# Pooling the opening's chunks in another way: strided reductions, split loads and a new order

## The chip, the cores and the metric

The kernel runs on one core of one Trainium2 chip. The metric is the device time of one execution in microseconds; several executions are timed and their median is given. A separate profile of one execution supplies the trace that the text reads: what each engine did, when, and what it waited for. The engines are TensorE (PE, with its weight loads as PEld), VectorE (DVE), ScalarE (ACT), GpSimd (POOL) and SyncE (SP), which here only issues transfers.

## The reference

An attention with spatially reduced keys is followed by a gated feed-forward layer:

```python
# q (4, 12288, 128), kv (4, 384, 32, 128), w_sr (128, 128)
kv_pool = kv.reshape(B, H // 4, 4, W // 4, 4, C).mean(axis=(2, 4))
k = v = kv_pool.reshape(B, -1, C) @ w_sr            # 768 keys for each image
s = (q @ k.transpose(0, 2, 1)) / np.sqrt(C)
a = softmax(s)                                       # over the 768 keys
x = (a @ v).reshape(B * N, 128)                      # 49152 tokens
out = (np.maximum(x @ w_gate, 0) * (x @ w_val)) @ w_out   # d_ff = 1536
```

Everything is float32 at the boundary; the kernel works in fp16 behind the loads and accumulates in fp32.

## The kernel before

The 49152 tokens are cut into 96 tiles of 512. The keys of an image are pooled in six chunks of 128 keys each; two chunks make a pair, and a pair is loaded as four lines (line dh holds the rows with that offset in the 4x4 pooling window; each partition gets 2 chunks x 4 pixels x 128 channels). One key of a chunk is thus the sum of 16 pieces: 4 lines x 4 pixels.

A tile goes through scores (TensorE), exponentials (ScalarE), values times weights (TensorE), 12 value projections `v`, 12 gate projections `g`, their copies `y` (value out of PSUM, ScalarE) and `h` (ReLU gate times value, VectorE), and 12 output matmuls `o`. From tile 4 on, a loop runs over the tiles as a pipeline; in each round a list of words (FIRST, then STEADY, at the end DRAIN and LAST) gives the order of the steps. The schedule is manual: each engine executes its instructions in the order in which the words issue them, and semaphores hold an engine until its operands are there.

The first four tiles (0 to 3, `LEAD`) and the keys of image 0 are made in the opening, the list OPENING, one call of `open_step` for each word. A dot separates two numbers. The words that matter here:

- `aJ`, `bJ`, `cJ`: sum two lines of chunk J, then add a third, then a fourth (512 elements a partition, `sum_lines`). `pJ`: sum pixels 0 and 1 with 2 and 3 (`sum_pixels`).
- `TJ.n`: TensorE turns the four pixels of line n of chunk J and adds them into one PSUM bank (`turn_add`; a matmul against the identity, so turning and adding is one step, 4 instructions); `TJ.p` does so with the two pieces left by `pJ`.
- `kvTJ`: the turned chunk is copied to SBUF; `pjJ`: projection by w_sr; `keyJ`: the keys scaled to fp16; `vtJ`, `valJ`: the same turned back as values.
- `castI`, `qtI`, `qTI`: a q tile cast to fp16, turned on TensorE, copied from PSUM; for tiles 4 and 5 the turn is a transposing transfer on SP's queue.
- `Sk.J`: scores of tile k against chunk J (one 512-wide matmul) and their exponential on ScalarE. `Vk.J`: the values of chunk J times these weights, added into tile k's bank. `xTk`: that bank copied out as fp16.
- `U0`, `U1`: matmuls with ones give the row sums of the four tiles, 24 matmuls of 32 columns each in all; `R`: VectorE transposes these sums and inverts them, and GpSimd copies the squares into `lead_scale`, 16 copies. `lead_scale` is needed when the output of tile 0 is scaled, near the end of the first round of the loop.
- `v0.n`, `g0.n` (tile 0): value projection with its copy, gate projection with its gate.
- `gateN`, `W0`, `W1`, `wo`: GpSimd waits for line N mod 4 of chunk N / 4, then issues the loads of the feed-forward weights.

ENGINES names the engine of a step (a ScalarE, v VectorE, p GpSimd; VectorE where nothing is named). PSUM has eight banks, taken from a list and given back in the order of the words (`bank`, `freed`, line 107); an instruction that writes a bank waits for the last reader of its former contents. The last words of OPENING may take only six banks, since the other two become the wide score bank of the loop. Before the opening, `fill(5)` runs five fp32 matmuls on the identity while the first lines are under way (L615).

Loads are issued in this order on SP's queue (lines 1 and 3 of pair 0 on ScalarE's): the lines of pair 0, w_sr, q tiles 0 and 1, line 0 of pair 1, q tiles 2 and 3, lines 1 to 3 of pair 1, the four lines of pair 2, q tiles 5 and 4. An issue waits for the landing of the transfer eight before it. After OPENING, GpSimd reads the last gated block of tile 0 into `gate` (L699) and issues the q loads of group 2 (L144).

Of the kernel before, what the change touches and what calls it, by code (L numbers as in the profile page):

```python
# [9 lines left out]
FP32 = mybir.dt.float32  # L10
FP16 = mybir.dt.float16
AF = mybir.ActivationFunctionType
ALU = mybir.AluOpType
# [3 lines left out]
def kernel(  # L17
# [48 lines left out]
    ENGINES = dict(word.split(":") for word in """  # L66
        key0:a val0:a a1:p kvT1:a key1:a val1:a key2:a val2:a a3:p b3:p p3:p kvT3:a val3:a
        cast0:a cast1:a qT1:a cast3:a cast4:p cast5:p xT1:a xT3:a
    """.split())
    OPENING = """  # L70
        T0.1 T1.3 cast1 T0.3 cast0 T1.2 T0.2 a1 p1 T1.p T0.0 kvT1 kvT0 pj1 qt1 pj0 T2.0 qT1 a3
        key1 cast3 qt0 cast2 vt1 qT0 key0 S1.1 qt2 qt3 qT2 val1 qT3 S1.0 S0.1 T2.1 S0.0 vt0 val0
        V1.1 S2.0 b3 c3 S2.1 S3.0 S3.1 T2.2 V0.1 T2.3 V1.0 kvT2 V2.1 V0.0 p3 gate22 W0 W1 cast4
        qT4 wo cast5 qT5 pj2 V2.0 T3.p T5.0 key2 vt2 kvT3 val2 pj3 key3 S0.2 T5.1 vt3 val3 S2.3
        a4 S0.3 S1.2 S2.2 T5.2 V0.2 S3.2 b4 V2.3 T5.3 V0.3 c4 S1.3 kvT5 S3.3 pj5 p4 T4.p V1.2
        key5 kvT4 V1.3 S0.5 pj4 key4 S2.5 vt5 val5 V2.2 S0.4 vt4 val4 S2.4 V0.5 V3.0 S1.4 V0.4
        S3.4 xT0 S1.5 V2.5 V2.4 S3.5 xT2 v0.5 g0.5 U0 v0.2 U1 v0.0 R g0.2 v0.3 V1.4 V3.1 g0.0
# [19 lines left out]
    """.split()  # L97
    SUMS = [{}, {"a": [0, 1]}, {}, {"a": [0, 1], "b": ["s", 2], "c": ["s", 3]}, {"a": [0, 1], "b": ["s", 2], "c": ["s", 3]}, {}]

# [16 lines left out]
    def freed(ps):  # L116
        free_banks.append(bank_numbers.pop(id(ps))[0])
        return ps
# [90 lines left out]

    def kv_load(b, pair, lines=range(r), queues=(nc.sync,)):  # L210
# [12 lines left out]
        rows = kv[b, pair * 2 * HC : (pair + 1) * 2 * HC].rearrange(  # L223
            "(hp dh) (wp h dw) c -> dh hp wp (h dw c)", dh=r, h=2, dw=r
        )
        for dh in lines:
            queues[dh % len(queues)].dma_start(
                parts[dh].rearrange("p h dw c -> p (h dw c)"), rows[dh]
            )

# [16 lines left out]
    def line(chunk, dh):  # L247
        return kv_in[0, chunk // 2][dh][:, chunk % 2]
# [3 lines left out]
    def add(name, to, x, y):  # L252
        engine_of(name).tensor_tensor(to, x, y, op=ALU.add)
# [6 lines left out]
    def sum_pixels(name, chunk):  # L260
        s1 = sums.pop(chunk)
        pixels[chunk] = work.tile([128, 2, C], FP32, tag="kv_c2", bufs=2, name="kv_c2")
        add(name, pixels[chunk], s1[:, 0:2], s1[:, 2:4])

    def turn_add(chunk, lines):
# [72 lines left out]
    hTs, o_banks, o_sbs, vals = {}, {}, {}, {}  # L338

    def scores(k, jc):  # L340
        if k not in aTs:
            aTs[k] = work.tile([128, NJC, T], FP16, tag="aT", bufs=AT_BUFS, name="aT")
        s_ps = bank([128, T])
        nc.tensor.matmul(s_ps, kv16[:, k // NST, jc, 0:C], qT_of(k), start=True, stop=True)  # L344
        nc.scalar.activation(aTs[k][:, jc, :], freed(s_ps), AF.Exp, scale=qk_scale)

# [79 lines left out]

    def lead_sums(chunks):
        if "sums" not in x_banks:
            x_banks["sums"] = bank([128, T])
        for jc in chunks:  # L430
            for k in range(LEAD):
                nc.tensor.matmul(  # L432
                    x_banks["sums"][32 * k : 32 * (k + 1), :], ones, aTs[k][:, jc, :],
                    start=jc == 0, stop=jc == NJC - 1, skip_group_check=True,
                    tile_position=(0, 32 * k),
                )

    def lead_scales():
# [21 lines left out]
    def keep_value(k, fb):  # L460
        vals[k, fb] = work.tile([128, T], FP16, tag="val", bufs=6, name="val")
        (nc.vector.tensor_copy if k < LEAD - 1 and fb == 5 else nc.scalar.copy)(  # L462
            vals[k, fb], freed(proj_banks.pop(("v", k, fb)))
        )
# [125 lines left out]

    w_sr_f32 = const.tile([128, C], FP32)
    kv_load(0, 0, range(r), (nc.sync, nc.scalar))
    nc.sync.dma_start(w_sr_f32, w_sr)
    q_load_pair(0)
    kv_load(0, 1, range(1))
    q_load_pair(2)
    kv_load(0, 1, range(1, 4))
    kv_load(0, 2)
    q_load_tile(5)
    q_load_tile(4)  # L600

# [16 lines left out]

    fill(5)
    freed(idle)  # L620

    gate = const.tile([128, 1], FP32)
    done = set()

    def open_step(word):
        head = "T" if word[0] == "T" else word.rstrip("0123456789.")
        at = [int(x) for x in word[len(head):].split(".") if x] if head != "T" else []
        if head in ("a", "b", "c"):
# [5 lines left out]
        elif head == "r":  # L634
            c2 = pixels[at[0]]
            add(word, c2[:, 0], c2[:, 0], c2[:, 1])
        elif head == "T":
            j, part = word[1:].split(".")
            turn_add(
                int(j), line(int(j), int(part)) if part.isdigit() else  # L640
                pixels.pop(int(j))[:, 0 : 2 if part == "p" else 1],
            )
# [16 lines left out]
        elif head == "S":  # L659
            scores(*at)  # L660
            done.add(tuple(at))
        elif head == "V" and at[0] < LEAD:
# [3 lines left out]
        elif head == "U":  # L666
            lead_sums(range(at[0] * (NJC - 1), NJC - 1 + at[0]))
        elif head == "R":
            lead_scales()
        elif head == "v":  # L670
            value_proj(*at)
            keep_value(*at)
        elif head == "g":
            gate_proj(*at)
            gated(*at)
        elif head == "W":
# [132 lines left out]
```

## Time and profile before

| What | us |
|---|---|
| median of 3 runs (1026.32 to 1027.2) | 1026.94 |
| span of the profiled execution, first to last instruction | 1024.5 |
| TensorE busy in that span | 1019.4 |
| ScalarE busy | 919.9 |
| VectorE busy | 861.8 |
| GpSimd busy | 524.8 |
| first matmul of FIRST (a value projection of tile 1) | 36.44 |
| last exponential of the opening ends | 28.88 |

The page gives busy time by engine over the whole span. Matmuls are pipelined and their ends are modelled, so TensorE's busy time counts a matmul until its result is there; the step from one matmul to the next is shorter. A row of the order of time reads: start, duration, engine, line, operation, tile written <- tile read, shape, count, and in brackets the idle time before it with what ended it. A row of a group reads: line, engine, operation, tiles, shape and count, then busy us and mean ns of one, then the idle time before them and what ended it. A row of a stretch gives its bounds and length, then the busy time of each engine with the number of instructions, the clock that TensorE was granted, the share of the DMA engines, and GB/s.

Lines of pair 0 land, by the trace, at 6.22 (line 0), 4.96 (1), 8.86 (2) and 8.65 (3); w_sr at 9.04, the first q pair at 10.31, line 0 of pair 1 at 11.59, the second q pair at 12.87, lines 1 to 3 of pair 1 at 14.14, 15.43 and 16.71, the lines of pair 2 at 17.99, 19.26, 20.55 and 22.22.

### The profile page before, as it was taken

The page shows a single profiled execution, that of the slowest core. Times are in us where ns is not written, and L with a number is a line of the kernel's source. Part 1 is how long each engine was busy: PE and PEld are TensorE (multiplying, and loading weights), DVE is VectorE, ACT ScalarE, POOL GpSimd, SP SyncE. Part 2 cuts the span into 40 slices and gives each one's busy share as a digit, 9 for nine tenths or more (in the row PEclk, how much of TensorE's full clock was granted, in tenths as well). Part 3 has the DMA queues.
Part 4 walks back from the last instruction along what each step waited for, and adds up shares of the span by engine and source line. Part 5 has one row for each costly group of instructions (what it writes and reads, how often), then busy time and mean ns, then how long its engine had stood idle before and what let it go on. Part 6 is the DMA issues. An engine that isn't in the chain of part 4 may idle for free.

```text
span 1024.5 us, 17514 instructions
## 1 busy us (share of the span) xinstructions
PE 1019.4 (100%) x5048; PEld 489.5 (48%) x5048; DVE 861.8 (84%) x1432; ACT 919.9 (90%) x1931; POOL 524.8 (51%) x1308
## 2 busy tenths in 40 slices
PE   9999999999999999999999999999999999999998
PEld 5444444444444444444444444444444444444445
DVE  2888888888888888888888888888888888888888
ACT  5999999989999999899999999989999999999986
POOL 3588857344346586544434856654333543343342
DMA  9999999877998999869879899887686987867541
GB/s 330 159 173 184 176 183 159 151 131 120 139 184 168 189 186 164 143 115 146 128 126 211 160 180 194 157 138 134 118 139 108 145 134 119 129 115 123 102 87 45
DMA packets 475312, 153.49 MB, mean 150 GB/s; under 512 B 451536, under 2 KB 465360, under 8 KB 475216
## 3 DMA queue, kind: packets, MB, share of 16 engines
q1 hardware_dynamic: 453184, 126.08, 67.7%
q0 software_dynamic: 21600, 25.19, 15.9%
q10 hardware_dynamic: 432, 1.11, 0.3%
q8 instruction: 40, 0.66, 0.3%
q14 instruction: 56, 0.46, 0.1%
HBM read 53.94 MB, written 26.35 MB: 78 GB/s over the span
## 4 chain that ended last, share of the span: by engine, by line
PE 98%; DMA 1%; ACT 1%; SPq 0%; issue 0%
PE bank_ps L455 24%; PE bank_ps L468 24%; PE bank_ps L496 23%; PE bank_ps L401 12%; PE wide_ps L359 12%; DMA q<-in_q_dram 1%; PE bank_ps L482 1%; PE bank_ps L344 1%; PE bank_ps L418 1%; PE bank_ps L270 0%; PE wide_ps L302 0%; PE bank_ps L284 0%; ACT a L364 0%; ACT val L462 0%; PE bank_ps L432 0%
## 5 line engine op out<-in xcount | busy, mean ns | idle before, releaser
L476 DVE SCALAR_TENSOR_TENSOR hT<-bank_ps,val 128x512 f16<-128x512 f32 x1152 | 727.8, 680 | 105.4 <-PE bank_ps L468 83.7
L462 ACT CAST val<-bank_ps 128x512 f16<-128x512 f32 x1149 | 628.1, 595 | 45.4 <-PE bank_ps L455 24.9
L455 PE MATMUL bank_ps<-xT,wv 128*128 128x512 f16 x1152 | 420.5, 379 | 0.0
L468 PE MATMUL bank_ps<-xT,wg 128*128 128x512 f16 x1152 | 375.9, 379 | 0.0
L496 PE MATMUL bank_ps<-hT,wo 128*128 128x512 f16 x1116 | 348.4, 379 | 0.0
L364 ACT ACTIVATE a<-wide_ps 128x768 f16<-128x768 f32 x368 | 302.0, 821 | 44.0 <-PE wide_ps L359 43.9
L359 PE MATMUL wide_ps<-kv,qT 128*128 128x512 f16 x736 | 179.7, 326 | 0.1
L401 PE MATMUL bank_ps<-aT,kv 128*128 128x512 f16 x552 | 178.9, 379 | 0.0
L496 PEld LDWEIGHTS <-wo 128*128 128x128 f16 x1116 | 109.2, 98 | 131.9 <-issue 0.6
L468 PEld LDWEIGHTS <-wg 128*128 128x128 f16 x1152 | 112.7, 98 | 122.4 <-issue 0.2
L509 POOL TENSOR_TENSOR o_sb<-o_t,scale 128x512 f32<-128x512 f32 x89 | 93.2, 1047 | 145.9 <-issue 128.4
L455 PEld LDWEIGHTS <-wv 128*128 128x128 f16 x1152 | 112.7, 98 | 105.7 <-issue 1.2
L385 POOL COPY scale<-square 32x8 f32<-32x8 f32 x736 | 141.2, 192 | 28.6
L739 POOL DMA_DIRECT2D out_dram<-o_sb x216 | 134.8, 627 | 19.5 <-POOL o_sb L509 13.0
L378 POOL TENSOR_TENSOR square<-inverse 128x8 f32<-128x8 f32 x46 | 9.3, 202 | 255.6 <-DVE inverse L376 249.4
L359 PEld LDWEIGHTS <-qT 128*128 128x128 f16 x736 | 72.0, 98 | 87.1 <-issue 0.4
L409 DVE CAST xT<-bank_ps 128x512 f16<-128x512 f32 x92 | 63.6, 691 | 32.0 <-PE bank_ps L401 32.0
L401 PEld LDWEIGHTS <-kv 128*128 128x128 f16 x552 | 54.0, 98 | 65.1
L364 ACT ACTIVATION_READ_ACCUMULATOR a<-wide_ps 128x1 f32 x368 | 75.9, 206 | 0.0
L504 DVE STREAM_TRANSPOSE o_t<-bank_ps 128x512 f32<-128x512 f32 x93 | 65.4, 703 | 0.0
L144 POOL DMA_DIRECT2D q<-in_q_dram x84 | 46.7, 573 | 0.6 <-PE bank_ps L496 0.4
L237 POOL TENSOR_TENSOR s<-kv_in 128x512 f32<-128x512 f32 x36 | 45.1, 1284 | 0.7
(78 smaller groups left out, 204.9 us busy)
## 6 DMA issues: line engine op xcount, KB each, us to landing
kv_in<-in_kv_dram SPq DMA_DIRECT2D x42, 512.0 KB, 4.7
out_dram<-o_sb SPq DMA_DIRECT2D x177, 64.0 KB, 3.7
out_dram<-o_sb POOLq DMA_DIRECT2D x176, 64.0 KB, 4.2
q<-in_q_dram POOLq DMA_DIRECT2D x84, 128.0 KB, 5.8
aT<-a SPq DMA_TRANSPOSE x184, 4.3
kv_line<-in_kv_dram SPq DMA_DIRECT2D x4, 512.0 KB, 9.7
placed<-blocks SPq DMA_DIRECT2D x9, 128.0 KB, 2.7
kvT<-placed SPq DMA_DIRECT2D x36, 32.0 KB, 2.1
```

Of the source, the lines that this page charges most:

```text
L359: nc.tensor.matmul(s_ps[:, j0 * 128 : j1 * 128], qT, kv16[:, b, j0:j1, 0:C], start=True, stop=True)
L364: nc.scalar.activation(a16s[k][:, s, :], s_banks.pop(s)[:, 0:J], AF.Exp, scale=qk_scale, accum_out=a_sums[k // 2][:, k % 2, s : s + 1],)
L385: nc.gpsimd.tensor_copy(to[32 * b : 32 * (b + 1), :, :, j], squares[k // 2][32 * j : 32 * (j + 1)])
L401: nc.tensor.matmul(x_banks[k], kv16[:, k // NST, jc, C : 2 * C], aT[:, jc], start=first, stop=x_left[k] == 0,)
L455: nc.tensor.matmul(proj_banks["v", k, fb], wv16[:, fb * 128 : (fb + 1) * 128], xTs[k], start=True, stop=True,)
L462: (nc.vector.tensor_copy if k < LEAD - 1 and fb == 5 else nc.scalar.copy)(vals[k, fb], freed(proj_banks.pop(("v", k, fb))))
L468: nc.tensor.matmul(proj_banks["g", k, fb], wg16[:, fb * 128 : (fb + 1) * 128], xTs[k], start=True, stop=True,)
L476: nc.vector.scalar_tensor_tensor(hTs[k][:, fb, :], freed(proj_banks.pop(("g", k, fb))), 0.0, vals.pop((k, fb)), op0=ALU.max, op1=ALU.mult,)
L496: nc.tensor.matmul(o_banks[k], wo16[:, fb, :], hTs[k][:, fb, :], start=fb == 0, stop=fb == NFB - 1)
L504: nc.vector.transpose(o_t, freed(o_banks.pop(k)))
L509: nc.gpsimd.tensor_tensor(to, o_by, scale.to_broadcast([128, NS, 4, 32]), op=ALU.mult)
L739: queue.dma_start(*out_moves.pop())
```

## The change

Everything is in the opening of the kernel; the loop and its lists are the same.

- Pooling. A new word `dJ.n` has VectorE reduce the four pixels of line n of chunk J to one piece by `tensor_reduce` over a strided view (512 inputs, 128 outputs a partition); `dJ.s` does so with a sum of lines. `TJ.dn` then turns that one piece (1 instruction instead of 4), and `TJ.s` turns the four pixels of a sum. Eleven such reductions come in. `p` and `c` steps are no longer used.
- Sums of lines: chunk 0 (lines 0 and 1) and chunk 1 (0 and 1, then 2) on GpSimd; chunk 2 (0 and 1, then 2) and chunk 5 (0 and 1) on VectorE.
- Loads. Lines 2 and 3 of pair 2 are loaded in two halves each, first both halves of chunk 4, then those of chunk 5; the order is a list, LOADS.
- The words are finer: scores `S` and exponentials `E` are apart, and for tile 0 `v`, `y`, `g` and `h` are apart. A bank is given back at the word of its reader.
- The list OPENING is new throughout. The row sums are `Un`, one chunk each, and stand at its end, as does `R`; the square in `R` is made by GpSimd. ENGINES has q tiles 0, 2 and 3 copied out of PSUM by ScalarE (tile 1 by VectorE), and other engines for some keys and values.
- `fill(3)` instead of `fill(5)`. The last 18 words, not the last 8, are held to six banks. The weights' gate is line 3 of chunk 4 instead of line 2 of chunk 5.

```diff
     OPENING = """
-        T0.1 T1.3 cast1 T0.3 cast0 T1.2 T0.2 a1 p1 T1.p T0.0 kvT1 kvT0 pj1 qt1 pj0 T2.0 qT1 a3
-        key1 cast3 qt0 cast2 vt1 qT0 key0 S1.1 qt2 qt3 qT2 val1 qT3 S1.0 S0.1 T2.1 S0.0 vt0 val0
...
-        v0.1 v0.4 V1.5 g0.3 v0.9 v0.11 g0.4 g0.9 V3.4 v0.8 v0.10 g0.1 xT1 g0.8 V3.5 v0.7 g0.11
-        V3.3 v0.6 V3.2 g0.10 xT3 g0.7 g0.6
+        a1 a0 T0.2 b1 d1.3 T0.s T0.3 T1.d3 kvT0 d1.s cast0 pj0 cast1 T1.ds qt0 kvT1 qT0 qt1
+        d3.0 pj1 key0 qT1 vt0 S0.0 key1 T3.d0 S1.0 val0 E0.0 S0.1 cast2 S1.1 cast3 vt1 qt2 val1
+        V0.0 E1.1 qt3 d3.1 qT2 a2 T3.d1 qT3 V1.1 S2.1 T3.2 E1.0 b2 S3.1 E2.1 V1.0 d2.s S2.0
+        E3.1 S3.0 T3.3 d2.3 E2.0 T2.ds V3.1 kvT3 E3.0 T2.d3 pj3 kvT2 d4.0 V3.0 key3 pj2 E0.1
+        S3.3 T4.d0 key2 S2.3 E3.3 S1.2 a5 S2.2 E2.3 V0.1 S0.2 d4.1 E2.2 T4.2 S3.2 d5.s E1.2 vt2
+        gate19 W0 W1 T4.3 E3.2 val2 T4.d1 S1.3 d5.2 V1.2 E0.2 T5.ds vt3 V3.2 kvT4 E1.3 T5.d2
+        V0.2 d5.3 pj4 val3 S0.3 V3.3 key4 T5.d3 E0.3 vt4 S1.4 kvT5 S0.4 val4 E1.4 pj5 V0.3 V1.3
+        key5 E0.4 V1.4 S0.5 vt5 S1.5 E0.5 S3.5 val5 S2.5 V0.4 E1.5 V0.5 S2.4 E2.5 S3.4 xT0 V1.5
+        E2.4 V2.0 V2.5 xT1 v0.5 E3.4 v0.0 g0.5 y0.5 E3.5 g0.1 v0.1 y0.0 V3.4 h0.5 g0.0 y0.1
...
+        v0.11 g0.9 g0.11 y0.11 h0.8 g0.7 xT2 U2 U0 h0.11 U5 y0.7 U4 h0.9 U1 U3 h0.7 cast4 qT4
+        wo cast5 qT5 R
     """.split()
+    LOADS = "P0 w Q0 P1.0 Q2 P1.1 P1.2 P1.3 P2.0 P2.1 K4.2 K4.3 K5.2 K5.3 q5 q4".split()
...
+    SUMS = [{'a': [0, 1]}, {'a': [0, 1], 'b': ['s', 2]}, {'a': [0, 1], 'b': ['s', 2]}, {}, {}, {'a': [0, 1]}]
...
         for dh in lines:
+            to, line_rows = parts[dh].rearrange("p h dw c -> p (h dw c)"), rows[dh]
+            if half is not None:
+                own = slice(half * r * C, (half + 1) * r * C)
+                to, line_rows = to[:, own], line_rows[:, :, own]
+            queues[dh % len(queues)].dma_start(to, line_rows)
...
+    def reduce_pixels(chunk, part):
+        lines = sums.pop(chunk) if part == "s" else line(chunk, int(part))
+        reduced[chunk, part] = work.tile([128, 1, C], FP32, tag="kv_d", bufs=4, name="kv_d")
+        nc.vector.tensor_reduce(
+            reduced[chunk, part][:, 0], lines.rearrange("p w c -> p c w"),
+            axis=mybir.AxisListType.X, op=ALU.add,
+        )
...
-        nc.vector.tensor_tensor(square, inverse, inverse, op=ALU.mult)
+        nc.gpsimd.tensor_tensor(square, inverse, inverse, op=ALU.mult)
...
-    fill(5)
+    fill(3)
...
-        usable[0] = 8 if at < len(OPENING) - 8 else 6
+        usable[0] = 8 if at < len(OPENING) - 18 else 6
```

More of the change, by code (lines that the diff above doesn't have):

```diff
@@ L66 @@
     ENGINES = dict(word.split(":") for word in """
-        key0:a val0:a a1:p kvT1:a key1:a val1:a key2:a val2:a a3:p b3:p p3:p kvT3:a val3:a
-        cast0:a cast1:a qT1:a cast3:a cast4:p cast5:p xT1:a xT3:a
+        cast4:p cast5:p a1:p a0:p b1:p kvT0:a cast0:a cast1:a qT0:a key0:a cast3:a qT2:a qT3:a
+        kvT2:a key3:a val3:a key4:a y0.5:v xT3:a xT2:a
     """.split())
     OPENING = """
-        T0.1 T1.3 cast1 T0.3 cast0 T1.2 T0.2 a1 p1 T1.p T0.0 kvT1 kvT0 pj1 qt1 pj0 T2.0 qT1 a3
-        key1 cast3 qt0 cast2 vt1 qT0 key0 S1.1 qt2 qt3 qT2 val1 qT3 S1.0 S0.1 T2.1 S0.0 vt0 val0
@@ L73 @@
[L73 to L77, printed above, removed]
-        v0.1 v0.4 V1.5 g0.3 v0.9 v0.11 g0.4 g0.9 V3.4 v0.8 v0.10 g0.1 xT1 g0.8 V3.5 v0.7 g0.11
@@ L208, with kv_load @@
     kv_in = {}
-    def kv_load(b, pair, lines=range(r), queues=(nc.sync,)):
+    def kv_load(b, pair, lines=range(r), queues=(nc.sync,), half=None):
         if (b, pair) not in kv_in:
@@ L338 @@
     hTs, o_banks, o_sbs, vals = {}, {}, {}, {}
+    score_ps = {}
     def scores(k, jc):
@@ L425, in lead_kept, with lead_sums @@
         copy_on(name, xTs[k], freed(x_banks.pop(k)))
-    def lead_sums(chunks):
+    def lead_sums(jc):
         if "sums" not in x_banks:
[L429 to L436, printed above, removed]
+            x_banks["sums"], x_count["sums"] = bank([128, T]), 0
+        x_count["sums"] += 1
+        for k in range(LEAD):
+            nc.tensor.matmul(
+                x_banks["sums"][32 * k : 32 * (k + 1), :], ones, aTs[k][:, jc, :],
+                start=x_count["sums"] == 1, stop=x_count["sums"] == NJC, skip_group_check=True,
+                tile_position=(0, 32 * k),
+            )
     def lead_scales():
@@ L660, in open_step @@
             scores(*at)
-            done.add(tuple(at))
+        elif head == "E":
+            exponentials(*at)
         elif head == "V" and at[0] < LEAD:
```

60 lines of the change are left out of this document (34 added, 26 removed).

## The prediction

> **What bounds the kernel now.** I read the page first, then busy time by stretch, then the order of time of the first 46 us, and last the groups of 0 to 36 us with shapes kept apart. From the page (first line: busy time by engine; second: the chain that ended last) and from three stretches (length, then busy us of PE, PEld, DVE, ACT, POOL):
>
> ```profile
> PE 1019.4 (100%) x5048; PEld 489.5 (48%) x5048; DVE 861.8 (84%) x1432; ACT 919.9 (90%) x1931; POOL 524.8 (51%) x1308
> PE 98%; DMA 1%; ACT 1%; SPq 0%; issue 0%
> ```
>
> ```profile
> 0.00:36.44 36.44, 34.68 (x202) 19.81 (x203) 16.15 (x36) 23.86 (x52) 15.74 (x41) 1.00 0.93 266
> 36.44:56.00 19.56, 19.44 (x93) 9.07 (x93) 18.59 (x31) 19.19 (x41) 8.94 (x17) 1.00 1.03 197
> 56.00:1024.50 968.50, 965.30 (x4755) 460.62 (x4752) 827.05 (x1367) 876.83 (x1840) 500.12 (x1251) 1.00 0.84 144
> ```
>
> TensorE binds from 56 us on; from 36.44 to 56 ScalarE is as full (19.19 of 19.56). The change touches only what lies before 36.44 us, where the first matmul of FIRST runs. So the question is when TensorE, and with it ScalarE, get there; a shift passes to the end one for one, since behind it no engine has room. The order of time of the opening (start, duration, engine):
>
> ```profile
> 2.37 0.34 PEld L615 LDWEIGHTS bank_ps<-ident 128*128 128x128 f32 x1 [0.52 <-issue]
> 3.23 0.34 PEld L615 LDWEIGHTS bank_ps<-ident 128*128 128x128 f32 x1 [0.52 <-issue]
> ...
> 6.78 0.19 PEld L615 LDWEIGHTS bank_ps<-ident 128*128 128x128 f32 x1 [0.24 <-issue]
> 7.21 0.19 PEld L615 LDWEIGHTS bank_ps<-ident 128*128 128x128 f32 x1 [0.24 <-issue]
> ...
> 8.07 2.59 PE L270 MATMUL bank_ps<-ident,kv_in 128*128 128x128 f32 x20
> ...
> 8.70 1.73 PEld L270 LDWEIGHTS bank_ps<-ident,kv_in 128*128 128x128 f32 x16 [0.26 <-DMA kv_in<-in_kv_dram]
> ...
> 13.77 0.61 ACT L345 ACTIVATE aT<-bank_ps 128x512 f16<-128x512 f32 x1
> ...
> 24.83 4.05 ACT L345 ACTIVATE aT<-bank_ps 128x512 f16<-128x512 f32 x8 [0.34 <-PE bank_ps L344]
> ...
> 29.99 1.73 ACT L462 CAST val<-bank_ps 128x512 f16<-128x512 f32 x3 [1.12 <-PE bank_ps L455]
> ...
> 36.27 0.66 ACT L126 CAST xT<-bank_ps 128x512 f16<-128x512 f32 x1
> ...
> 36.44 0.38 PE L455 MATMUL bank_ps<-xT,wv 128*128 128x512 f16 x1
> ```
>
> Real work on TensorE begins at 8.07, the first exponential at 13.77, the last ends at 28.88, ScalarE ends the opening at 36.93. The fill matmuls come every 0.86 us at first and every 0.43 us from 6.35 on. And the groups (shape, count, busy us, mean ns):
>
> ```profile
> L345 ACT ACTIVATE aT<-bank_ps 128x512 f16<-128x512 f32 x24 | 12.6, 621 | 0.8 <-PE bank_ps L344 0.7
> ...
> L253 POOL TENSOR_TENSOR kv_s<-kv_in 128x512 f32<-128x512 f32 x2 | 2.5, 1264 | 10.9 <-DMA kv_in<-in_kv_dram 10.9
> ...
> L253 DVE TENSOR_TENSOR kv_s<-kv_s,kv_line 128x512 f32<-128x512 f32 x2 | 1.4, 692 | 0.9 <-DMA kv_line<-in_kv_dram 0.9
> ...
> L442 DVE RECIPROCAL inverse<-sums_turned 128x16 f32<-128x16 f32 x1 | 0.3, 253 | 0.0
> ```
>
> **TensorE's account.** Steps: a transpose of pooling 0.108 us (1.73 for 16), a 512-wide matmul 0.216, a projection 0.29, a 128-wide fp16 transpose 0.055, one row-sum matmul 0.06 (1.19 for 20 on the chain). Before: 62 transposes 6.7, 72 wide matmuls 15.55, 6 projections 1.74, 22 small ones 1.2, 24 sums 1.44: 26.6 of the 28.37 us between 8.07 and 36.44, so 1.7 idle. After: chunk 0 turns 12 pieces, chunk 1 two, chunk 2 two, chunks 3 and 4 ten each, chunk 5 three: 39, 23 fewer, -2.5 us. The first transpose now is line 2 of pair 0, which lands at 8.86 (before, TensorE began with line 1, long there): +0.9. If nothing waited, FIRST would begin at 8.95 + 24.1 = 33.1.
>
> **ScalarE's account.** To the last exponential it has 3 casts (0.57), 2 kvT (0.26), 3 qT instead of 1 (0.585), 3 keys and 1 value instead of 3 and 4 (0.28), 24 exponentials (0.525): 17.7 us. It starts with kvT0 instead of a cast. That needs line 3 turned at 10.43, so it begins at 10.48 against 10.33: 28.2 without waits. Two waits are in its order. From qT0 and key0 (12.74) over S0.0 to E0.0 it waits 0.5; its E0.0 then stands at 13.3, half a microsecond earlier than the first exponential before. Near the end E0.5 waits for kvT5, pj5, key5 and S0.5, 0.4 to 0.6. Where a fresh key or cast is the weight operand, the trace has 0.05 us to the load and 0.17 to the matmul, not 0.05 alone: four such places, 0.3. Last exponential at 29.3 (before 28.88). Then 11 vals (0.55) and 2 xT (0.61), 7.3 us, with no wait like the 1.12 us in front of the first vals before, because v0.5 and v0.0 stand ahead of the last exponentials: end at 36.6 (before 36.93).
>
> **VectorE's account.** Eleven tensor_reduce come in, of 512 inputs each; four sums (0.69) and two half sums (0.42) go and three sums (0.69) come. No row shows a tensor_reduce. Nearest are the 512-input sums, 0.69; below, 0.42 of a 256-input sum cannot hold twice the inputs; above, the strided reciprocal, 0.253 for 16 against 0.192 for 8 (another shape), gives 7.6 ns per element, far off and an iterated operation; twice the input time, 1.2, is the upper end that I keep. I take 0.69: +7.6 and -1.5, about 6 us more, where VectorE was idle for 20 of 36 us. In its queue, by landing times: d1.3 8.75 to 9.44; d1.s behind GpSimd's b1; kvT1, d3.0, qT1, key1, val0, cast2, val1 to 14.3; then d3.1, a2, b2, d2.s, d2.3, kvT3 without a gap to 18.3; d4.0 to 19.0, a gap of 0.6 until key2, and full again to d5.3 at 23.8. What it issues is just in time: kvT2 is wanted by ScalarE at 18.8 and its transpose is there at 18.4. So 0.69 costs nothing, and each 0.1 more per reduce is half absorbed.
>
> **GpSimd, early.** a1 6.37 to 7.63, a0 to 8.90, b1 to 10.16 (1.264 each), in place of one sum then and two later. T0.s needs a0 at 8.90, when TensorE turns T0.2 anyway: nothing. d1.s needs b1: 10.21 to 10.90, and T1.ds 0.1 later: 0.3 of TensorE's early waits.
>
> **Loads.** Same bytes and order; lines 2 and 3 of the last pair come as four halves in place of two lines. Landings lie 1.28 us apart per line, so chunk 4 is whole at 20.55 and chunk 5 at 22.2, as before. Small pieces could land worse: the 64 KB q pieces came every 0.23 us, which for a half of 256 KB would be 0.9 instead of 0.64, the last at 23.2. d5.3 is free to start at 23.1, so 0 to 0.2. The two further issues on SP's queue wait for landings that are past anyway; q5 and q4 follow with the same last issue, tied to the landing at 22.2. The weights' gate hangs on a piece of 20.55, as before.
>
> **The tail.** Sums U and R move behind everything. TensorE's g0.7 wants a bank that y0.9 frees, at 34.9; then 24 sums, 1.44: FIRST at 36.5 to 36.8, against 36.44. VectorE, after the last gate at 37.5, does R's transpose (0.72) and reciprocal (0.25) to 38.4, and its first val of FIRST stood at 38.65: nothing. On GpSimd the square (0.2), 16 copies (3.65), the gate and four q loads (2.17) are behind it: done at 44.7 instead of 39.25, landed near 49 instead of 44.15. SP's transpose of that q, at 48.24 before, waits about 1 us, and behind it stores and aT transposes; SP waited 3.3 us for ScalarE at 52.29, which takes that up. cast4 to cast5 keep their places on GpSimd.
>
> **Sum.** TensorE: start +0.9, work -2.5, waits 3.6 in place of 1.7, rounded +0.3 at FIRST (36.7); ScalarE there -0.3, then fed 0.2 later than now. I take +0.3. The profiled execution has a span of 1024.5, which lies 2.4 below the median of 1026.94 (what is around the span); 1026.94 + 0.3 = 1027.2. Its own range, from 29.3 and 36.7 being off by a microsecond of waits, is 1026.2 to 1028.6. A measurement of this kernel can tell about 0.2% (2.05 us) from no change.
>
> **Rivals.**
> *Half-rate TensorE (slower).* With fill at 3, TensorE stops at 6.4, stands until 8.95, and is sparse to 15. Rows: fills take 0.86 before 6.35 and 0.43 behind, so a slow rate exists and lasts some 5 us of work, though PEclk says 1.00. If it returns or never left, 12 transposes take 2.6 instead of 1.3, ahead of ScalarE's first kvT0: +1.3; if it lasts to the first scores, pj0, qt0, qt1 and S0.0 add some 0.9 and slower answers to 16 us the rest: up to +2.6. So 1028.5 to 1029.8; it decides for slower if the first exponential starts past 15.2. Against: a full 5 us of fills remain, and the standstill is 2.5 us. The Trainium skill, TensorE: Matmul & The Clock Gate (Part 1), says the clock doubles after one busy window of about 3.4 us and halves after an idle one, and that the windows run free of the kernel; the step at 6.35 agrees, and by it a standstill of 2.5 us keeps the rate, but 5 us of fills need not hold a whole window. Chance 0.26, of which 0.15 past 0.2%.
> *Slow tensor_reduce.* At 1.2 us each, VectorE's unbroken stretch pushes kvT3 by 2 and kvT5 by 3.3, ScalarE starves: 1029 to 1030.2. For it: inputs of one sum lie 512 bytes apart. The Trainium skill, SBUF — State Buffer (cachelines), says that each access to a new 16-byte line pays a penalty; no row here shows one, and by it this case holds. Chance 0.12, 0.09 past 0.2%.
> *Queues stay fed.* If early waits shrink to the 1.7 of now, ScalarE's own work (25.0 from 10.48) still ends at 35.5, 1.5 earlier: 1025.4, and past 1024.9 only if FIRST also gains. Chance 0.14, 0.07 past 0.2%.
> *Late R.* If SP's wait reaches aT or the kv lines, 1 to 3 us: 1028 to 1030. Chance 0.05, 0.03 past 0.2%.
> Forecast 0.43, 0.03 past 0.2% slower. Sums: faster 0.07, slower 0.30, within 0.63. Leaving out a tenth at each side: 1025.2 to 1029.9.
>
> **What will show it.** 39 transposes of pooling; first kvT0 on ScalarE at 10.5 and first exponential at 13.3 (half rate: past 11.7 and 14.6); tensor_reduce at 0.69; last exponential at 29.3; FIRST's first value matmul at 36.7; q loads of group 2 on GpSimd from 42.5. Wrong if ScalarE has gaps over 1.5 us between 13.3 and 29.3, or if TensorE in the 19.56 us behind FIRST's start stands longer than the 0.4 of now (its 93 matmuls there, 75 by 0.216 and 18 by 0.163, make 19.1).

## The result and the profile after

The changed kernel takes 1031.08 us (median of 9 runs, 1027.03 to 1032.66) against 1026.88 (9 runs, 1026.23 to 1027.21) for the kernel before. It is slower by 4.2 us in the medians and by 3.4 in the means (1030.13 against 1026.78); the ratio, 1.0033 with a 95% interval of 1.0025 to 1.0041, agrees with the means. The forecast of 1027.2 with its range to 1029.9 is missed. The nine runs lie further apart than those of before (5.6 us against 1.0), which is itself a trace of the cause.

Each run is listed with its mean granted clock of TensorE. Seven of the nine runs show 0.997 or 0.998, two 1.000, and the profiled run is one of these two; of the 88 runs of the kernel before that have this figure only one is under 0.999. One step of 3.41 us at half rate makes 0.998. So the profile below shows the changed kernel without a loss that most of its runs have; the experiments come back to it.

The profiled execution took 1031.27 us, with a span of 1029.5. From its page, busy time by engine and the chain that ended last:

```profile
PE 1017.1 (99%) x5021; PEld 485.9 (47%) x5021; DVE 870.6 (85%) x1440; ACT 921.4 (90%) x1930; POOL 524.6 (51%) x1308
PE 95%; DMA 3%; DVE 1%; ACT 0%; POOL 0%; issue 0%; POOLq 0%
```

TensorE is busy 2.3 us less than before, with two fills and 23 transposes fewer, and yet the span is 5.0 longer. On the chain DMA has 3% instead of 1%, and VectorE's 1% is new. Three stretches as for the kernel before, from the start of the kernel to FIRST, some 20 us more, and the rest; the second bound, 57.00 for 56.00, is set so that about the same TensorE work lies behind it (length, then busy us of PE, PEld, DVE, ACT, POOL, then clock, DMA share, GB/s):

```profile
0.00:37.38 37.38, 32.18 (x176) 16.34 (x176) 24.61 (x44) 24.91 (x51) 12.11 (x24) 1.00 0.95 265
37.38:57.00 19.62, 19.51 (x98) 9.18 (x95) 18.62 (x32) 18.95 (x40) 11.04 (x31) 1.00 0.89 127
57.00:1029.50 972.50, 965.39 (x4754) 460.43 (x4751) 827.37 (x1367) 877.55 (x1840) 501.47 (x1253) 1.00 0.83 145
```

Read the lengths. The opening is 0.94 us longer (37.38 against 36.44). The third stretch is 4.0 us longer (972.5 against 968.5) with the same TensorE work in it (965.4 against 965.3), though not a line of the loop was changed. So in this run one fifth of the loss is made where the change is, and four fifths far behind it. TensorE's waits from 36 us to the end show what they are; the kernel before has no such row (columns: engine, tile and line, releaser: us in total, times, longest):

```profile
PE bank_ps L424 <- DMA aT<-a: 4.0, 2, 2.0
```

Twice TensorE stands about 2 us for the transfer that turns the weights `a` of a tile. Set side by side by its value projections, the kernel is late by 0.94 us at FIRST and 0.8 from 40 to 100 us; the lateness jumps to 2.9 at about 105 us and to 5.1 at about 180, and stays there to the end. The chain at the first jump:

```profile
94.77 11.13 DMA aT<-a
105.89 0.14 issue
106.03 0.38 PE bank_ps L424
```

This is the tenth transfer of aT, and the second stall waits for the 24th. Their rows in both kernels (times of issue; "first use" is the matmul that reads the transfer):

| transfer of aT | kernel | q loads of a group from | transfer: issue, landing | first use |
|---|---|---|---|---|
| tenth | before | 90.31 | 87.54, 94.53 | 103.14 |
| tenth | after | 94.42 | 94.77, 105.89 | 106.03 |
| 24th | before | 167.39 | 163.76, 167.83 | 176.56 |
| 24th | after | 170.27 | 170.57, 181.52 | 181.66 |

In the kernel before each of the two landed some 8.7 us ahead of its use. In the changed kernel each was issued about 7 us later, for a reason that SyncE's queue shows further down, and took longer too: 11.1 us instead of 7.0, and 11.0 instead of 4.1. That it took longer goes with its new place: it had been issued 2.8 and 3.6 us ahead of the four q loads of a group on GpSimd, and now comes 0.3 us behind the first of them. In the kernel before the 21 aT transfers issued within 4 us behind such loads took 7.4 us in the median, the other 163 took 4.1. The sum for the tenth: landed 11.4 later, less 8.6 of margin and the 0.9 by which TensorE was late already, leaves 1.9, the stall.

The opening itself went as forecast on TensorE and ScalarE up to the first exponential, and then lost a microsecond. In order of time (start, duration, engine):

```profile
8.52 1.05 DVE L277 TENSOR_REDUCE kv_d<-kv_in 128x128 f32<-128x512 f32 x1 [7.65 <-DMA kv_in<-in_kv_dram]
8.89 0.66 PE L287 MATMUL bank_ps<-ident,kv_in 128*128 128x128 f32 x4 [2.05 <-DMA kv_in<-in_kv_dram]
...
10.46 0.27 ACT L131 COPY kvT_chunk<-bank_ps 128x128 f32<-128x128 f32 x1 [6.91 <-PE bank_ps L287]
...
13.28 0.60 ACT L366 ACTIVATE aT<-bank_ps 128x512 f16<-128x512 f32 x1 [0.54 <-PE bank_ps L363]
...
24.86 0.28 ACT L306 ACTIVATE kv<-bank_ps 128x128 f16<-128x128 f32 x1 [0.78 <-PE bank_ps L301]
...
27.37 3.05 ACT L366 ACTIVATE aT<-bank_ps 128x512 f16<-128x512 f32 x6 [0.44 <-PE bank_ps L363]
...
37.38 0.39 PE L478 MATMUL bank_ps<-xT,wv 128*128 128x512 f16 x1
...
39.32 3.66 POOL L470 COPY lead_scale<-square 32x16 f32<-32x16 f32 x16
...
43.58 2.23 POOL L149 DMA_DIRECT2D q<-in_q_dram  x4 [0.35 <-ACT val L486]
```

The first kvT0 stands at 10.46 (forecast 10.48) and the first exponential at 13.28 (13.3). A tensor_reduce takes 1.05 us, not 0.69. The six exponentials that start at 27.37 end at 30.42, where 29.3 was forecast. On GpSimd the q loads of group 2 stand behind `R`'s 16 copies, from 43.58 on; before, they were issued from 37.08 on.

SyncE's queue shows what that does to the transfers (start, duration, queue), first in the kernel before, then in the changed one:

```profile
48.24 1.31 SPq L155 DMA_TRANSPOSE qT<-q  x1
...
51.10 1.09 SPq L739 DMA_DIRECT2D out_dram<-o_sb  x2
52.29 3.30 SPq L391 DMA_TRANSPOSE aT<-a  x1
```

```profile
46.95 3.39 SPq L414 DMA_TRANSPOSE aT<-a  x1
53.59 1.34 SPq L160 DMA_TRANSPOSE qT<-q  x1
...
58.22 4.78 SPq L414 DMA_TRANSPOSE aT<-a  x1
```

The turn of q (line 160, formerly 155) is issued at 53.59, where it was at 48.24 before, because the last of the late q loads landed at 53.44 instead of 44.15. The aT transfers before and after it lie as follows:

| transfer of aT, in order | before: issue, landing | after: issue, landing |
|---|---|---|
| second | 46.17, 50.18 | 46.95, 61.60 |
| third | 52.29, 59.75 | 58.22, 65.88 |
| fourth | 59.84, 65.11 | 66.38, 71.90 |
| fifth | 64.46, 69.79 | 71.91, 76.92 |
| sixth | 67.87, 72.26 | 75.77, 79.51 |

The second takes 14.6 us instead of 4.0: it was issued right behind the q loads. From the third on they are 6 to 7 us late, while TensorE is only 0.8 us late. Nothing waits for them yet, since the weights are made well ahead; but the margin is spent, and the tenth transfer, which takes long, finds TensorE standing.

### The profile page after: what moved, and what is told of

The parts are those of the page before. It is cut to its first block, busy times and chain, and to the rows that moved or that the text cites. A ratio compares the mean times of both kernels' runs of the same rounds, so it can differ in the third digit from the quotient of the medians.

```text
span 1029.5 us, 17464 instructions
## 1 busy us (share of the span) xinstructions
PE 1017.1 (99%) x5021; PEld 485.9 (47%) x5021; DVE 870.6 (85%) x1440; ACT 921.4 (90%) x1930; POOL 524.6 (51%) x1308
## 4 chain that ended last, share of the span: by engine, by line
PE 95%; DMA 3%; DVE 1%; ACT 0%; POOL 0%; issue 0%; POOLq 0%
PE bank_ps L478 24%; PE bank_ps L492 24%; PE bank_ps L520 23%; PE bank_ps L424 11%; PE wide_ps L382 11%; DMA aT<-a 2%; DVE kv_d L277 1%; PE bank_ps L506 1%; DMA kv_in<-in_kv_dram 1%; POOL kv_s L260 0%; PE bank_ps L441 0%; PE wide_ps L319 0%; PE bank_ps L363 0%; DVE kv_s L260 0%; ACT a L387 0%
```

## The experiments

Unless said otherwise a kernel is the changed one with the edit shown. Times are medians, each against runs of the kernel before on the same chip. The theory to be tested first was that of the late q loads; its rivals were the cost of the opening alone, and TensorE's clock.

**The q loads ahead of R.** The square and its 16 copies go behind the loads on GpSimd; no other step moves.

```diff
-        wo cast5 qT5 R
+        wo cast5 qT5
...
-        usable[0] = 8 if at < len(OPENING) - 18 else 6
+        usable[0] = 8 if at < len(OPENING) - 17 else 6
...
     q_load(2)
+    open_step("R")
```

> The changed kernel with one order changed on GpSimd: the gate and the four q loads of group 2 stand ahead of R's square and 16 copies, no longer behind them; every other engine keeps its list. Theory (late q loads: they land 9 us later than before, SP's turn of that q waits for them, all aT transfers behind it run 7 us late, and TensorE stalls twice for 2.1 us, at 105 and 178): the q loads are issued near 37 and land by 46, the third aT transfer is issued near 53 instead of 58.2, no stall, the runs agree within 1 us, and what is left is the opening's 0.8: 1027.5 to 1027.9. Rival (the two further transfers on SP's queue shift which landing each issue waits for): that shift is still in, so 1028 to 1032 with the same spread. Rival (TensorE's clock): the same, 1028 to 1032.

Measured: 1027.94 (11 runs, 1026.79 to 1028.8) against 1026.98, ratio 1.0010 (1.0001 to 1.0018). Of the 4.2 us 3.2 are gone (of the 3.4 in the means 2.4), and so is TensorE's wait for aT in the profiled run. The place of these loads decides most of the loss. What is left there is another thing. Four stretches of that run, two microseconds each (columns as above):

```profile
6.00:8.00 2.00, 0.10 (x1) 0.00 (x0) 0.00 (x0) 0.00 (x0) 1.43 (x2) 1.00 1.02 416
8.00:10.00 2.00, 0.92 (x5) 0.93 (x6) 1.04 (x1) 0.00 (x0) 1.89 (x2) 0.66 1.06 418
10.00:12.00 2.00, 2.00 (x10) 1.71 (x9) 1.04 (x1) 0.07 (x1) 0.44 (x1) 0.50 1.02 406
12.00:14.00 2.00, 1.71 (x14) 1.07 (x13) 1.11 (x2) 1.98 (x5) 0.00 (x0) 0.99 1.04 414
```

The granted clock is 0.66 and 0.50 where the profiled run of the changed kernel has 1.00. From 8.62 to 12.03 us TensorE ran at half rate, behind a standstill of 2.98 us (the fill ended at 6.10, the next matmul began at 9.08). The four transposes of the sum take 1.06 us here and 0.60 there:

```profile
9.98 1.06 PE L287 MATMUL bank_ps<-ident,kv_s 128*128 128x128 f32 x4
...
11.94 0.27 ACT L131 COPY kvT_chunk<-bank_ps 128x128 f32<-128x128 f32 x1 [8.38 <-PE bank_ps L287]
```

kvT0 follows at 11.94 instead of 10.46, the first exponential at 14.51 instead of 13.28, FIRST at 38.50. This is the rival of the half-rate TensorE. In the profiled run of the changed kernel the fill had ended later (6.85), the standstill was 2.05 us, and the clock stayed. That run is the exception: ten of the eleven runs of this experiment show a mean granted clock of 0.997 or 0.998, and the one with 1.000 is the shortest (1026.79; the others begin at 1027.56). The stretches of the first microseconds need care here: the clock records of a trace begin only when full rate is reached (5.21 us in this run, 7.04 in the changed kernel's profile, none in that of the kernel before), and what lies in front is printed as 1.00, though the fill matmuls there come at half pace, every 0.86 us.

**The kernel before, with its q loads late.** 34 small copies on GpSimd stand in front of the loads and do nothing else.

```diff
     nc.gpsimd.tensor_copy(gate, hTs[0][:, NFB - 1, 0:1])
+    held = const.tile([128, 16], FP32)
+    for n in range(34):
+        nc.gpsimd.tensor_copy(held[0:32], gate[0:32].to_broadcast([32, 16]))
     q_load(2)
```

> The kernel before with 34 idle copies of 32x16 on GpSimd between the gate and the q loads of group 2, so that these are issued near 43.8 instead of 37.1; nothing else. Theory (late q loads): the aT transfers run 5 to 7 us late as in the changed kernel, and stalls of about 2 us appear: 1028 to 1031, with runs further apart than the 1 us of before. Rivals (shifted landings, clock, or a cause in the opening): no stall, 1026.9.

Measured: 1037.98 (6 runs, 1033.04 to 1045.7) against 1026.98, ratio 1.011 (1.0081 to 1.0139). The loads were issued from 46.0 to 47.7, later than forecast and than in the changed kernel, the third aT transfer at 63.41 instead of 52.29. TensorE's waits, where the kernel before has none:

```profile
PE bank_ps L401 <- DMA aT<-a: 5.4, 2, 3.2
PE bank_ps L401 <- DVE hT L476: 1.0, 1, 1.0
```

With the old opening and the old pooling, late loads bring the same kind of loss (by the times of the kernel before the lateness of TensorE jumps at 73, 157 and 178 us), and later loads than those of the changed kernel bring more of it. The copies hold all that GpSimd does behind them, not the loads alone, and one wait of 1.0 us is for VectorE; the first experiment, which moves only the loads and `R` against each other, has no such doubt.

**Tensor_reduce over adjacent inputs.** The view is changed so that the four inputs of a sum lie side by side instead of 512 bytes apart. It then sums neighbouring channels and leaves out the sum over pixels; only its times are of use.

```diff
-            reduced[chunk, part][:, 0], lines.rearrange("p w c -> p c w"),
+            reduced[chunk, part][:, 0], lines.rearrange("p w c -> p (w c)").rearrange("p (c w) -> p c w", w=r),
```

> The changed kernel with every tensor_reduce taking four adjacent elements instead of four that lie 512 bytes apart (the same 512 inputs and 128 outputs, and a wrong pooling: it sums neighbouring channels and not pixels). If the distance is what makes 1.03 us of 0.69: 0.69 each, and FIRST begins at 36.7 instead of 37.4. If tensor_reduce itself has that rate: 1.03 each, FIRST at 37.4. By the theory of late q loads the stalls stay either way: 1027 to 1032.

Measured: 1028.43 (12 runs, 1026.09 to 1033.06) against 1026.98, ratio 1.0020 (1.0008 to 1.0032). The groups of 0 to 40 us on VectorE, first of the changed kernel, then of this one (count, then busy us and mean ns):

```profile
L277 DVE TENSOR_REDUCE kv_d<-kv_in 128x128 f32<-128x512 f32 x4 | 4.1, 1030 | 7.7 <-DMA kv_in<-in_kv_dram 7.7
...
L277 DVE TENSOR_REDUCE kv_d<-kv_line 128x128 f32<-128x512 f32 x4 | 4.1, 1027 | 0.0
```

```profile
L277 DVE TENSOR_REDUCE kv_d<-kv_in 128x128 f32<-128x512 f32 x4 | 2.7, 680 | 7.8 <-DMA kv_in<-in_kv_dram 7.8
...
L277 DVE TENSOR_REDUCE kv_d<-kv_line 128x128 f32<-128x512 f32 x4 | 2.7, 676 | 0.0
```

The stride costs 0.35 us per instruction. The Trainium skill, SBUF — State Buffer, says in its note on cachelines that each access that crosses to a new 16-byte line pays a penalty; 0.68 against 1.03 us agrees with it. If that is the cause, which no run separates from other costs of a stride, the penalty adds a half to the instruction's time here. FIRST stood at 36.78, 0.6 earlier than in the changed kernel, although the clock was halved in this profiled run (8.44 to 11.85). The stalls for aT are there still (3.9 us in two), so the strided reductions are not what makes them.

**The fill of before.** `fill(5)` in place of `fill(3)`.

```diff
-    fill(3)
+    fill(5)
```

> The changed kernel with fill(5) as before. Theory (late q loads): the opening is the same, FIRST at 37.4, the stalls stay, 1027 to 1032 with the same spread. Rival (half-rate TensorE in some runs): all runs then have a warm opening, the spread falls under 1 us and the time to about 1027.7.

Measured: 1031.45 (5 runs, 1029.03 to 1032.86) against 1026.98, ratio 1.0038 (1.0026 to 1.0050). No gain over the changed kernel as long as the loads are late. The profiled run, at 1029.03 the shortest of them, had one stall for aT:

```profile
PE bank_ps L424 <- DMA aT<-a: 1.6, 1, 1.6
```

**Both: loads ahead of R and fill(5).** The edits of the first and of the fourth experiment together.

> The changed kernel with two things undone: the q loads of group 2 stand ahead of R on GpSimd (as in e1_loads_first), and fill(5) instead of fill(3). Theory (three terms that add: tensor_reduce at 1.03 us delays the opening, half-rate TensorE behind the standstill from 6.1 to 9 adds 1.2 in most runs, late q loads add up to two stalls of 2): only the first is left. No stretch of the opening at a granted clock below 1, FIRST at 37.4, no stall, 1027.0 to 1027.7, runs within 1 us. Rival (fill is of no account): same median as e1_loads_first, 1027.9.

Measured: 1026.96 (11 runs, 1026.78 to 1027.54) against 1026.69, ratio 1.0004 (0.9995 to 1.0013). The loss is gone but for 0.3 us, and the runs lie as close together as those of before. All eleven runs show a mean granted clock of 1.000. The profiled run has FIRST at 37.49, and its last value projection is 0.9 later than in the kernel before: the opening's own microsecond, passed to the end and no more. SyncE's queue in it, to be read against that of the changed kernel above:

```profile
47.06 1.77 SPq L414 DMA_TRANSPOSE aT<-a  x1
49.01 1.32 SPq L160 DMA_TRANSPOSE qT<-q  x1
...
53.33 4.33 SPq L414 DMA_TRANSPOSE aT<-a  x1
```

The turn of q is issued at 49.01 and the third aT transfer at 53.33, 4.6 and 4.9 us earlier than there.

**Half sums in place of the reductions.** On top of the last kernel each tensor_reduce becomes one sum of pixels 0 and 1 with 2 and 3, and TensorE turns the two pieces left.

```diff
-        reduced[chunk, part] = work.tile([128, 1, C], FP32, tag="kv_d", bufs=4, name="kv_d")
-        nc.vector.tensor_reduce(
-            reduced[chunk, part][:, 0], lines.rearrange("p w c -> p c w"),
-            axis=mybir.AxisListType.X, op=ALU.add,
-        )
+        reduced[chunk, part] = work.tile([128, 2, C], FP32, tag="kv_d", bufs=4, name="kv_d")
+        nc.vector.tensor_tensor(reduced[chunk, part], lines[:, 0:2], lines[:, 2:4], op=ALU.add)
```

> As e5_first_fill5, and each of the eleven tensor_reduce is replaced by one sum of two pixels with two (256 outputs, 0.42 us by the rows of before), whose two pieces TensorE turns: 11 transposes more, 1.2 us of TensorE, 6.7 us less of VectorE. Theory (VectorE's queue sets the opening): kvT3 and kvT5 come earlier, FIRST at 35.7 to 36.4, 1025.6 to 1026.6, below the kernel before. Rival (TensorE's own work sets it): FIRST 1 us later than in e5_first_fill5, 1028.

Measured: 1026.27 (11 runs, 1025.49 to 1027.39) against 1026.69, ratio 0.9994 (0.9986 to 1.0003). The sums take 0.42 us each:

```profile
L277 DVE TENSOR_TENSOR kv_d<-kv_line 128x256 f32<-128x256 f32 x4 | 1.7, 421 | 0.7 <-DMA kv_line<-in_kv_dram 0.7
```

FIRST comes at 35.89, 1.6 earlier than with the reductions and 0.55 earlier than before, and the last value projection of the profiled run is 0.7 earlier. That is the best opening of all. In the time it can't be told from the kernel before, but the spans tell it: their median is 1023.9 us against 1024.9, and eight of the eleven lie below every one of the 33 spans of the kernel before. The time around the span, 1.7 to 1.9 us in those 33 runs, is up to 3.0 in some runs of this kernel; why is open.

**Whole lines for pair 2.** On top of the kernel with both edits, the last pair is loaded as four lines again.

```diff
-    LOADS = "P0 w Q0 P1.0 Q2 P1.1 P1.2 P1.3 P2.0 P2.1 K4.2 K4.3 K5.2 K5.3 q5 q4".split()
+    LOADS = "P0 w Q0 P1.0 Q2 P1.1 P1.2 P1.3 P2.0 P2.1 P2.2 P2.3 q5 q4".split()
```

> As e5_first_fill5, with lines 2 and 3 of the last pair loaded whole again (both land at 20.6 and 22.2 instead of chunk 4's halves at 20.0 and 20.6). If the halves matter: T4.3 waits for 22.2, and with it everything behind it on TensorE, and the weights' gate too: FIRST 0.5 to 1 us later than in e5_first_fill5. If they do not: the same time within 0.3 us.

Measured: 1027.33 (11 runs, 1027.02 to 1029.66) against 1026.69, ratio 1.0009 (1.0000 to 1.0018). FIRST at 37.70 against 37.49, the median 0.4 higher: the halves cost nothing that shows, and are worth 0.2 to 0.4 us at the most; the intervals of the two ratios overlap.

**The kernel before with fill(3).**

```diff
-    fill(5)
+    fill(3)
```

> The kernel before with fill(3) instead of fill(5) and nothing else. Theory (a standstill behind too few fills brings half rate): TensorE turns line 1 at 6.5 and then waits for 8.65; half rate in many runs, 20 transposes at 0.22 instead of 0.11: 1028 to 1029, runs further apart. Rival (the fills do not matter, the standstill of the new order does): 1026.9.

Measured: 1026.87 (11 runs, 1026.11 to 1027.36) against 1026.69, ratio 1.0002 (0.9993 to 1.0010). No change, and no half rate in the profiled run. There TensorE turns line 1 at 6.64 to 7.6, so that its standstill is only 1.1 us. So the shorter fill costs something only together with the later first transpose that the new opening brought.

The last three experiments ask by which way the late loads delay the aT transfers: SyncE's queue stands at the turn of q until they land; or the transfers slow each other when the loads of two groups and the aT transfers meet; or the DMA engines lose the 4 us in which nothing was issued. All three start from the changed kernel with fill(5), and keep the loads late.

**The turn of q later on SyncE's queue.**

```diff
-        if ph % 2:
+        if ph % 2 and k != GRP + 1:
             q_turn_two(g + 1, ph - 1)
+        if k == GRP + 2:
+            q_turn_two(2, 0)
```

> As e4_fill5 (late q loads kept, half rate excluded), but SP's first turn of group 2 is issued one round later, behind the aT transfers of its round, so that SP no longer stands until the late q has landed. Theory A (SP's queue in order: what stands behind the waiting turn is 7 us late from then on): the third aT transfer is issued near 53 instead of 57.6, later ones as in e5_first_fill5, no stall, 1027.0 to 1027.7. Theory B (the transfers themselves: the q loads of groups 2 and 3 now run together and hold up the aT transfers beside them): the second aT transfer still lands near 61, the stalls stay, 1029 to 1032.

Measured: 1031.75 (6 runs, 1029.06 to 1033.51) against 1026.56, ratio 1.0041 (1.0029 to 1.0054). The third aT transfer is issued at 54.32 instead of 58.22, but its row on SyncE's queue lasts 8.06 us, it lands at 66.30, and the second still takes from 47.36 to 62.47. SyncE's wait alone is not the way.

**The q loads of group 3 a round later.**

```diff
-        if ph == 1:
+        if ph == 1 and k != GRP + 1 or k == GRP + 2:
             q_load(g + 2)
```

> As e4_fill5, but the q loads of group 3 are issued one round later, so that those of group 2 (still late, near 44) run without them. Theory A (SP's wait for the late q): the turn still waits until 52 to 53, the third aT transfer is still issued past 56, stalls stay: 1029 to 1032. Theory B (transfers against each other): the second aT transfer lands by 53 instead of 61, later ones less late, few stalls: 1027 to 1028.5.

Measured: 1029.55 (12 runs, 1027.49 to 1035.43) against 1026.56, ratio 1.0032 (1.0020 to 1.0043). With fewer loads beside it the second aT transfer takes 8.3 us (47.18 to 55.44) instead of 14.6, and the third is issued at 57.34. Stalls remain; the profiled run was the longest of the twelve:

```profile
PE bank_ps L424 <- DMA aT<-a: 6.0, 3, 2.8
```

**Both of these.**

> As e4_fill5 with both moves at once: SP's first turn of group 2 one round later (e9_turn_later) and the q loads of group 3 one round later (e10_loads_apart); the q loads of group 2 are still issued near 44. Theory A and B together (a wait in SP's queue, and loads that jam the aT transfers; each alone is enough to stall): both gone, the second aT transfer lands by 55, the third is issued by 54, no or few stalls, 1027 to 1028. Theory C (the DMA engines stand for 4 us, 40 to 44, with a share of 0.04 instead of 0.97, and are behind by that much work wherever it is put): the work is only put off, stalls stay, 1029 to 1032.

Measured: 1028.13 (11 runs, 1026.76 to 1032.77) against 1026.76, ratio 1.0018 (1.0000 to 1.0035). The third aT transfer is back at 53.35, and in the profiled run (1027.59) TensorE does not wait for aT. Five of eleven runs lie at or below 1027.6, as with early loads, the others reach up to 1032.8. Late loads with fill(5) cost 4.5 us (1031.45 against 1026.98), so most of the loss goes, not all. The interval is wide, also because one of the 15 runs of the kernel before took 1033.54 us, the only one of its 97 runs above 1028. The third way may hold the rest. The stretch of 40 to 44 us, in the changed kernel, in this one, in the one with early loads and fill(5), and in the kernel before:

```profile
40.00:44.00 4.00, 4.00 (x21) 1.85 (x19) 4.00 (x8) 3.89 (x9) 3.08 (x15) 1.00 0.04 9
```

```profile
40.00:44.00 4.00, 4.00 (x21) 1.87 (x20) 4.00 (x8) 3.89 (x9) 3.04 (x16) 1.00 0.03 8
```

```profile
40.00:44.00 4.00, 4.00 (x21) 1.94 (x20) 4.00 (x8) 3.89 (x9) 3.12 (x17) 1.00 0.97 174
```

```profile
40.00:44.00 4.00, 4.00 (x21) 1.95 (x20) 4.00 (x7) 3.83 (x9) 0.00 (x0) 1.00 1.08 161
```

The DMA share is 0.04 and 0.03 where the loads are late, 0.97 and 1.08 where they are not. Four microseconds of the DMA engines are lost there, in a kernel whose later share is 0.83: what is to be moved is moved later, beside the next transfers. That this carries the rest is argued and not shown: no run filled the hole while the loads stayed late.

## Why the prediction was wrong

**The step that failed** is "The tail". It placed the cause where it is: the four q loads behind the square and the 16 copies on GpSimd, SP's transpose of q behind their landing, the aT transfers behind that. Then it costed it at nothing, because SP waited 3.3 us for ScalarE at 52.29, "which takes that up". No run shows that slack, and three more things in the step were off.

- The 3.3 us are the length of the third aT transfer's own row on SP's queue. It begins at 52.29, and the row in front ends at 52.19, so nothing was waited for between them. Had it been a wait for ScalarE, a later issue would have shortened it: issued 5.9 us later it lasted 4.78 us, while ScalarE was less than 1 us late. So the delay of the queue passed on whole: the turn of q 5.35 us late, the third aT transfer 5.93.
- The loads were to land "near 49"; the last landed at 53.44. They were issued 1.1 us later than forecast, of which 0.7 comes from FIRST, and the forecast took their former time to land, though the path they now met was another.
- SP's transpose was to wait "about 1 us"; it was issued 5.35 us later than before (53.59 against 48.24).
- The transfer issued just behind the loads was not looked at. The second aT transfer took 14.6 us instead of 4.0, and this lies beside SP's wait, not in it: moving the turn of q out of the way alone did not help (1031.75). Nor did the text follow the late queue further, to the tenth and the 24th transfer, which now come behind a group's q loads instead of ahead of them.

The rival "Late R" had the mechanism and the end (its "1 to 3 us: 1028 to 1030"), though with a chance of 0.05 and too small a price. Undoing this one order took the loss from 4.2 us to 1.0, and loads held back by copies on GpSimd made the kernel before 11.0 us slower. The two account for the main part of the result as cause; how it divides between SyncE's wait, transfers against each other and the lost 4 us is open. Where the stalls fall is read from the rows of the tenth and the 24th transfer; no run moved these two alone.

**TensorE's account** had the start right: kvT0 at 10.46 for 10.48, first exponential 13.28 for 13.3. Its 2.5 us less of work can't be read off the busy time. Of the 2.3 us there, two fills fewer make 1.4 (6.88 to 5.49 us), and the real work up to FIRST 1.2 (27.97 to 26.76), since a lone transpose counts 0.30 us as busy and not the step of 0.108. By the account's own sum, 8.89 + 24.1 leaves 4.4 us of waits before 37.38, where it put 3.6.

**VectorE's account** was mis-sized: 1.03 us per tensor_reduce, not 0.69. The nearest row by inputs was a sum of adjacent operands, and the stride was held to the upper end. By "each 0.1 more per reduce is half absorbed" the text would have given 1.9 us for eleven at 0.34 more; the last exponential was 1.1 late and FIRST 0.7, so more was absorbed than that. Adjacent inputs alone brought FIRST 0.6 earlier. The rival "Slow tensor_reduce" asked for 1.2 us and 1029 to 1030.2; against half sums the reductions' own part is 0.7 us in the medians of the time, 1.3 in those of the span, 1.6 at FIRST.

**The half-rate rival** happens, and in most runs of the new opening with fill(3): ten of eleven with early loads, none of eleven with early loads and fill(5). In seven of the nine runs of the changed kernel the clock was below 0.999 too, by the opening or by stalls. It had a chance of 0.26. Its mark, kvT0 past 11.7 and the first exponential past 14.6, is nearly met in the profiled run of the first experiment (11.94 and 14.51), the last value projection there 1.0 us later than with fill(5) (1.9 against 0.9 behind the kernel before), for a forecast of 1.3. In the medians fill(5) brings 0.7 (1.0 above before without it, 0.3 with it). The argument against it in the prediction, that 2.5 us of standstill would keep the rate, did not hold as a rule: 2.98 us were enough to lose it, and 2.5 of them had passed when the clock fell. The profiled run of the changed kernel, with 2.05 us, shows the kept rate, so its +0.94 at FIRST is without this cost.

**GpSimd early** and **Loads** were right: the reduction behind GpSimd's sums began at 10.29 for 10.21, the last halves of the two chunks landed at 20.64 and 22.42 for 20.55 and 22.2, and whole lines in their place made the kernel no faster. **The sum** of +0.3 at FIRST became +0.94, through VectorE. Two of its small terms don't add up, to little effect: ScalarE's own terms give 29.4 to 29.6 for the last exponential and not 29.3, and the time around the span is 1.8 us, not 2.4, since the profiled run was one of the shorter ones. The last sign that was named, TensorE's idle time in the 19.56 us behind FIRST, stayed small (0.11 of 19.62); the stall came 50 us further on, where the text did not look. "A shift passes to the end one for one" held for the opening's microsecond; that behind it "no engine has room" was read as if it could only pass a shift on, and a full pipeline can also add to it.

## What to carry to other kernels

When a step moves on an engine's queue, follow each transfer behind it to its landing, with what else is in flight then, and on to the consumer's margin: a delay that nobody waits for at first can be spent margin, and come due 50 us later as stalls. Runs of one kernel that lie further apart than those of another are a sign of such spent margins. Price a strided reduction by a row with that stride, or take the upper end; and check that warm-up work still reaches the first real work when either is moved.

## What the runs showed of the hardware

- A tensor_reduce of 512 fp32 inputs to 128 outputs takes 1.03 us with inputs 512 bytes apart, and 0.68 with adjacent ones; a sum of 256 and 256 takes 0.42.
- A transposing transfer on SyncE's queue that lands 4.0 us after its issue in the kernel before took 14.6 us when it was issued 1.1 us behind four loads of q on GpSimd's queue and the loads of the next group followed, and 8.3 us when these were put off by a round. Over the whole kernel before, aT transfers issued within 4 us behind a group's q loads took 7.4 us in the median, the others 4.1.
- TensorE's granted clock halves after a short standstill: with early loads at 8.62 us, 2.5 us after the last matmul of the fill, for 3.41 us. In the profiled runs every standstill of 2.79 us or more was followed by this step (six of them, 2.79 to 4.28), none of 2.14 us or less was. Stalls for aT were followed by the same step in the middle of the kernel (182.5 to 185.9 in the run with adjacent inputs, 109.9 to 113.3 in the one with the later turn), so that a stall can cost more than its length: with the later turn a stall of 4.28 us made TensorE 6.0 us later. The Trainium skill, TensorE: Matmul & The Clock Gate (Part 1), has the halving after an idle window of about 3.4 us. The length of the step agrees with that figure. The standstill that starts it does not: 2.79 us sufficed here, and the measurement decides.
